# Attention's score and value products spaced on PE, and the first expert weights issued from GpSimd in 1 KB rows

## The chip, the cores and the metric

One core of a Trainium2 chip. The metric is the device time of one execution in microseconds; of several runs of a kernel the median counts. The engines are TensorE (PE in the profile, with its weight loads as PEld), VectorE (DVE), ScalarE (ACT), GpSimd (POOL) and SyncE (SP, which here only starts DMA transfers).

## The reference, cut to what matters

Chunked attention with memory slots over 4 batches, 8 heads, 768 positions and head size 64; its output, as 3072 tokens of 512 numbers, goes through a layer of 8 experts whose shares P come from a Sinkhorn iteration.

```python
# attention: chunk 32, left 16, right 8, 8 memory slots, scale 1/sqrt(64)
for c in range(nc):
    l_start, r_end = max(0, c_start - 16), min(S, c_end + 8)
    k_full = concatenate([mem_k, k[:, :, l_start:r_end]], axis=2)
    v_full = concatenate([mem_v, v[:, :, l_start:r_end]], axis=2)
    scores = scale * (q[:, :, c_start:c_end] @ k_full^T)
    a = exp(scores - max(scores))
    out[:, :, c_start:c_end] = (a / (sum(a) + 1e-9)) @ v_full

# experts: x is (3072, 512), w1[e] (512, 1024), w2[e] (1024, 512)
P = exp(x @ w_gate - max(x @ w_gate))
for _ in range(8):
    P /= P.sum(1, keepdims=True) + 1e-9
    P /= P.sum(0, keepdims=True) + 1e-9
    P *= N / E
for e in range(8):
    out += P[:, e:e+1] * (maximum(x @ w1[e], 0) @ w2[e])
```

## The kernel before

**Tiling.** Attention works on blocks of 128 queries, 24 in all; for a block n PE transposes queries and keys (tq, tk, and now and then tx for extra keys kx), makes the scores (`sp`, 64 small fp32 products), DVE takes their maximum (sm) and subtracts it (s), ACT takes the exponential, PE transposes it (ta) and makes the values product (`xp`, 64 small products again), DVE divides (rec, xq) and PE transposes the result into token columns (xt). Four blocks make a unit of 512 tokens; there are six units. `build(u)` turns a unit's tokens into operands for the experts.

The experts' products run in fp16 on numbers split into a high and a low half, three passes for each product. A scale comes first: the maximum of a weight tile or of the tokens (DVE, `most`, L540 and L956), reduced over the partitions by PE (row_w, sp_w, row_x, sp_x); then ACT writes the high half (L495) and DVE the low half (L503). Most products of expert and unit use a scheme with seven products in place of eight (L1580: px, py, pz and, for the second layer, yx, yy, yz). Unit 0 of expert 0 uses plain products: `pp` (L2017) for the first layer and `yp` (L2098) for the second, because only sums and splits of plain weights are needed for them, and so they come first on PE. They need the first weights w1f of expert 0, four tiles of 512 KB (fp = 0 to 3), and the tokens of blocks 0 to 3.

**The order of the work.** Nothing is issued where the Python stands. Every step is a `Task` with an engine, a cost in microseconds, a priority (small goes first) and its dependencies; a `Plan` then simulates all engines with these costs and takes, again and again, the task that can start earliest, and among those that could start already the one with the smallest priority number. The program of each engine is the order that comes out of it. Each transfer has a cost in that plan too: one clock `dma` for all queues, pushed on by the transfer's `dma` number. Where PE would stand still by the plan for more than 0.4 us, `pad` puts filler products into PE's program (L409, `warm`, a 128 x 256 product on the identity that nobody reads):

```python
if t.eng == "PE" and self.fill is not None and at - clock["PE"] > 0.4:
    self.pad(clock["PE"], at)
```

The priorities at the head of the program are numbers written by hand: `BLOCKS = (-50.0, -44.0, -30.0, -26.0)` for the four blocks of unit 0, `VALUES` for their values, and `FIRST = (-38.0, -20.0)` for the first layer's and the second layer's weights of expert 0. `fetch_first(1, START)` loads the four tiles of w1, takes their maxima and makes their scale; `plain1` splits them. All loads but a few of ACT are issued by SyncE (`eng="SP"`), one after the other, and a w1 tile is two of them (fh = 0 and 1), each of 256 KB in rows of 512 bytes:

```python
for fh in range(2):
    queue.dma_start(st.t[:, fh], w1v[e, fp, :, :, fh])
```

In `hidden()`, which makes the first layer by the scheme of seven products, every product waits for all pieces of its two operands (`made = wmade + xmade`).

Of the kernel before, what the change touches and what calls it, by code (L numbers as in the profile page):

```python
# [24 lines left out]
BEHIND = 5.0  # L25
FIRST = 2.0
MARGIN = 8.0
FAR = 60.0


class Task:


    __slots__ = ("eng", "cost", "fn", "prio", "left", "ready", "end", "then", "takes", "frees", "n", "dma", "start")
# [55 lines left out]
class Plan:  # L90
# [8 lines left out]
    def __init__(self):  # L99
        self.tasks = []  # L100
        self.free = {}
        self.fill = None

    def add(self, eng, cost, fn, deps=(), prio=0.0, bufs=(), takes=None, frees=None, dma=0.0):
        t = Task()
        t.eng, t.cost, t.fn, t.prio, t.takes, t.frees = eng, cost, fn, prio, takes, frees
        t.ready, t.end, t.then, t.n, t.dma = 0.0, None, [], len(self.tasks), dma
        if dma:
            t.cost = cost * ISSUE
# [23 lines left out]

    def run(self):
# [3 lines left out]
        dma = FIRST  # L138
# [4 lines left out]
        while left:  # L143
            best = None
            for e in self.ENGINES:
# [5 lines left out]
                pick = None  # L151
                for _, _, t in sorted(a):
                    if t.takes is None or self.free.get(t.takes.group):
                        at = now
                        if t.takes is not None:
                            at = max(at, self.free[t.takes.group][0][0])
                        if pick is None or at < pick[0]:
                            pick = (at, t, a)
                        if at <= now:
                            break  # L160
                for r, _, t in sorted(w)[:12]:
                    if pick is not None and r >= pick[0]:
                        break
                    if t.takes is None or self.free.get(t.takes.group):
                        at = r
                        if t.takes is not None:
                            at = max(at, self.free[t.takes.group][0][0])
                        if pick is None or at < pick[0]:
                            pick = (at, t, w)
# [15 lines left out]
            if t.dma:  # L185
                at = max(at, dma - BEHIND)
                t.start = at
                clock[t.eng] = at + t.cost
                dma = max(dma, at + t.cost / 2) + t.dma
                t.end = max(dma, at + t.cost) + 2.6  # L190
            else:
                clock[t.eng] = t.end = at + t.cost
            t.fn()
# [2106 lines left out]
```

## Time and profile before

| | us |
|---|---|
| median of 3 runs | 1922.85 |
| lowest and highest run | 1922.3 and 1923.82 |
| span of the profiled execution | 1921.2 |
| PE busy in it | 1905.9 |
| DVE, ACT and POOL busy in it | 1436.7, 1032.3 and 520.3 |

The profile is of one execution. A row of a timeline gives the start, the duration, the engine, the line, the operation, the tiles (out<-in) and how many instructions are taken together; the bracket at its end is the idle time of the engine just before, with what ended it. "issue" stands where an engine waited for nothing that the profile shows. PEclk is the granted clock of PE as a share of full speed: 1.00 is 2.4 GHz, 0.50 is 1.2 GHz. Rows of the views stand further down in numbered groups.

### The profile page before, as it was taken

What the parts mean: (1) busy time and instruction counts of PE and PEld (TensorE: products, weight loads), DVE (VectorE), ACT (ScalarE), POOL (GpSimd) and SP (SyncE); (2) the same over time, 40 slices, a digit from 0 to 9 for tenths busy, and PEclk for the clock granted to TensorE, in tenths of its full rate; (3) what the DMA queues carried; (4) which work ended last, traced back from release to release, by engine and by line L of the source; (5) the groups of instructions that cost most, each with busy time, mean ns of one, the idle gap of its engine ahead of it and who ended that gap; (6) DMA issues with size and microseconds to landing.
All of it is one profiled execution on the core that took longest, in us unless ns stands there. A gap on an engine that the chain in (4) does not pass through costs nothing.

```text
span 1921.2 us, 47293 instructions
## 1 busy us (share of the span) xinstructions
PE 1905.9 (99%) x19608; PEld 1641.5 (85%) x19608; DVE 1436.7 (75%) x2396; ACT 1032.3 (54%) x2019; POOL 520.3 (27%) x549
## 2 busy tenths in 40 slices
PE   8999999999999999999999999999999999999999
PEld 7676676688888888888888888888888888888888
DVE  5666569778769866897778875898678885786565
ACT  4665564556556545645545554654554564564453
POOL 1220002443224231432124231342124232332112
PEclk9999999999999999999999999999999999999999
DMA  8677653454235342255214533245313632322321
GB/s 197 174 202 205 169 162 122 138 176 144 83 103 173 131 138 94 78 178 186 109 57 148 204 105 127 78 160 171 143 45 99 242 128 92 102 83 83 127 83 67
DMA packets 246792, 254.82 MB, mean 133 GB/s; under 512 B 113265, under 2 KB 180273, under 8 KB 242225
## 3 DMA queue, kind: packets, MB, share of 16 engines
q1 hardware_dynamic: 244452, 251.21, 40.8%
q8 instruction: 153, 2.51, 0.5%
q10 hardware_dynamic: 2124, 0.59, 0.2%
q14 instruction: 63, 0.51, 0.1%
HBM read 187.84 MB, written 63.44 MB: 131 GB/s over the span
## 4 chain that ended last, share of the span: by engine, by line
PE 94%; DVE 3%; issue 1%; DMA 1%; ACT 0%; POOL 0%; SPq 0%; DVEq 0%; POOLq 0%
PE px L1580 26%; PE yx L1580 22%; PE pz L1580 13%; PE yz L1580 11%; PE py L1580 6%; PE yp L2098 6%; PE yy L1580 5%; PE xp L1119 1%; PE sp L1051 1%; PE pp L2017 1%; DVE ss L1738 1%; PE warm L409 1%; PE ta L1109 0%; PE tk L992 0%; PE tq L988 0%
## 5 line engine op out<-in xcount | busy, mean ns | idle before, releaser
L1580 PEld LDWEIGHTS <-w 128*128 128x128 f16 x7896 | 770.9, 98 | 93.1 <-issue 0.8
L1580 PEld LDWEIGHTS <-h 128*128 128x128 f16 x7056 | 689.9, 98 | 82.9 <-issue 2.6
L1580 PE MATMUL px<-x,w 128*128 128x256 f16 x4512 | 549.1, 273 | 0.5 <-issue 0.3
L1903 POOL TENSOR_TENSOR acc<-acc,y 128x256 f32<-128x256 f32 x252 | 265.6, 1060 | 862.4 <-ACT y L1878 839.8
L1580 PE MATMUL yx<-w,h 128*128 128x256 f16 x4032 | 467.6, 273 | 0.7 <-DVE acc L1913 0.6
L1629 ACT ACTIVATE q<-px 128x256 f32<-128x256 f32 x376 | 142.7, 381 | 304.4 <-PE px L1580 299.8
L1580 PE MATMUL pz<-x,w 128*128 128x256 f16 x2256 | 278.4, 273 | 0.0
L1580 PE MATMUL yz<-w,h 128*128 128x256 f16 x2016 | 233.8, 273 | 1.2 <-ACT y L1878 1.2
L1798 DVE TENSOR_TENSOR h<-ss,h 128x1024 f16<-128x1024 f32 x160 | 214.7, 1344 | 3.8 <-ACT h L1774 3.5
L1749 ACT ACTIVATE h<-c 128x768 f16<-128x768 f32 x168 | 140.8, 838 | 109.5 <-DVE c L1639 109.5
L1774 ACT CAST h<-ss 128x1024 f16<-128x1024 f32 x168 | 174.2, 1040 | 24.9 <-DVE ss L1738 24.0
L1738 DVE SCALAR_TENSOR_TENSOR ss<-c,ss 128x256 f32<-128x256 f32 x336 | 172.3, 513 | 8.2
L1782 DVE SCALAR_TENSOR_TENSOR h<-c,h 128x768 f16<-128x768 f32 x168 | 165.0, 982 | 11.2 <-ACT h L1749 11.2
L1639 DVE SCALAR_TENSOR_TENSOR c<-px,q 128x256 f32<-128x256 f32 x188 | 77.7, 421 | 94.2 <-PE px L1580 85.0
L1878 ACT ACTIVATE y<-yx,pscale 128x256 f32<-128x256 f32 x168 | 79.3, 473 | 112.6 <-PE yx L1580 108.8
L1580 PE MATMUL py<-x,w 128*128 128x256 f16 x1128 | 139.2, 273 | 0.0
L1639 DVE SCALAR_TENSOR_TENSOR c<-py,q 128x256 f32<-128x256 f32 x188 | 78.8, 422 | 72.1 <-PE py L1580 66.1
L2098 PE MATMUL yp<-w,h 128*128 128x512 f16 x576 | 131.7, 379 | 0.0
L1738 DVE SCALAR_TENSOR_TENSOR ss<-c,h 128x512 f32<-128x512 f32 x168 | 122.7, 730 | 2.2 <-ACT h L1726 2.2
L1580 PE MATMUL yy<-w,h 128*128 128x256 f16 x1008 | 116.9, 273 | 0.0
L2098 PEld LDWEIGHTS <-h 128*128 128x128 f16 x576 | 55.4, 98 | 58.9
L503 DVE SCALAR_TENSOR_TENSOR w<-ws,sw,w 128x1024 f16<-128x1024 f32 (+1 forms) x64 | 84.9, 1326 | 25.8 <-ACT w L495 25.8
(158 smaller groups left out, 1755.1 us busy)
## 6 DMA issues: line engine op xcount, KB each, us to landing
x<-xkeep SPq DMA_DIRECT2D x28, 1792.0 KB
akeep<-acc SPq DMA_DIRECT2D x168, 256.0 KB
acc<-akeep SPq DMA_DIRECT2D x168, 256.0 KB
w1f<-in_moe_w_dram SPq DMA_DIRECT2D x72, 256.0 KB
w2f<-in_moe_w_dram SPq DMA_DIRECT2D x32, 512.0 KB
w1fm<-in_moe_w_dram SPq DMA_DIRECT2D x56, 256.0 KB
w2fm<-in_moe_w_dram SPq DMA_DIRECT2D x28, 512.0 KB
xkeep<-x SPq DMA_DIRECT2D x6, 1792.0 KB
```

The source lines that it names most:

```text
L503: lambda: nc.vector.scalar_tensor_tensor(dst(1), src(), s, dst(0), op0=ALU.mult, op1=ALU.subtract),
L1580: nc.tensor.matmul(dst.t, a, b, start=(not more and n == 0), stop=(n == end), skip_group_check=more,)
L1629: lambda: nc.scalar.activation(t.t, src.t, AF.Copy, scale=DOWN),
L1639: lambda: nc.vector.scalar_tensor_tensor(c.t[:, o], src.t, DOWN, q.t, op0=ALU.mult, op1=ALU.add),
L1738: lambda: nc.vector.scalar_tensor_tensor(dst(), src(), 0.0, other(), op0=ALU.max, op1=op),
L1749: lambda: nc.scalar.activation(h.t[:, 0, 0:3], c.t, AF.Relu),
L1774: lambda: nc.scalar.copy(h.t[:, 0, 3:7], ss.t),
L1782: lambda: nc.vector.scalar_tensor_tensor(h.t[:, 1, 0:3].rearrange("p a n -> p (a n)"), c.t.rearrange("p a n -> p (a n)"), 0.0, h.t[:, 0, 0 ...
L1798: lambda: spare.tensor_tensor(h.t[:, 1, 3:7], ss.t, h.t[:, 0, 3:7], op=ALU.subtract),
L1878: (lambda: nc.scalar.activation(t.t, src.t, AF.Copy, scale=f))
L1903: lambda: nc.gpsimd.tensor_tensor(acc.t[:, cols], acc.t[:, cols], q.t, op=ALU.add),
L2098: nc.tensor.matmul(py.t, hf.t[:, hl, where[fh], o : o + P], room(fp, WIDE * wl + DM * fh, WIDE * wl + DM * (fh + 1)), start=(fp == 0 and i ...
```

## The change

Five things.

1. **Spacing.** The tasks of scores and values products from block 2 on are marked `many`. When one has been placed, the plan remembers its end plus 3.6 us (`again`). If the next pick on PE is such a task and would start before that, the plan takes another task in its place, if one could start no later than 0.1 us after it.
2. **First weights.** The four w1 tiles of expert 0 are issued by GpSimd, with priority -60 in place of -38, and their maxima and splits have earlier priorities. In the plan GpSimd's transfers have a clock of their own beside that of SyncE and ACT.
3. **Rows of 1 KB.** Every w1 tile is loaded as one transfer of 512 KB with rows of 256 numbers, in place of two with rows of 128. A tile holds other columns than before, so w2's rows are grouped to match, and the places inside the tiles follow (`place`, `source`, `tile1`).
4. **Block 1** has the priority -48 in place of -44 for its queries and keys.
5. **Waits in `hidden()`.** A product waits for the pieces of its operands that it reads.

The diff, cut:

```diff
+APART = 3.6
...
     def run(self):
...
-        dma = FIRST
+        dma = {"SP": FIRST, "POOL": FIRST}
...
+                pick = self.next(now, w, a, False)
+                if pick is not None and pick[1].many and pick[0] < self.again:
+                    other = self.next(now, w, a, True)
+                    if other is not None and other[0] <= pick[0] + 0.1:
+                        pick = other
...
             if t.dma:
-                at = max(at, dma - BEHIND)
+                own = "SP" if t.eng == "ACT" else t.eng
+                at = max(at, dma[own] - BEHIND)
...
+            if t.many:
+                self.again = t.end + APART
...
-    w1v = w1.rearrange("e (kt p) (fh fp f) -> e fp p kt fh f", p=P, fh=2, fp=FP)
-    w2v = w2.rearrange("e (fh fp p) d -> e fp p fh d", fh=2, fp=FP)
+    w1v = w1.rearrange("e (kt p) (fp f) -> e fp p kt f", p=P, fp=FP)
+    w2v = w2.rearrange("e (fp fh p) d -> e fp p fh d", fh=2, fp=FP)
...
-        queue = nc.scalar if eng == "ACT" else nc.sync
+        queue = {"ACT": nc.scalar, "POOL": nc.gpsimd, "SP": nc.sync}[eng]
...
-                for fh in range(2):
-                    queue.dma_start(st.t[:, fh], w1v[e, fp, :, :, fh])
+                queue.dma_start(st.t.rearrange("p k a f -> p k (a f)"), w1v[e, fp])
...
-        return st, add(eng, 2 if which == 1 else 1, go, after, prio, [st], dma=2.1)
+        return st, add(eng, 1, go, after, prio, [st], dma=2.1 if eng == "SP" else 2.8)
...
-    BLOCKS = (-50.0, -44.0, -30.0, -26.0)
+    BLOCKS = (-50.0, -48.0, -30.0, -26.0)
     VALUES = (-47.0, -41.0, -28.0, -24.0)
-    FIRST = (-38.0, -20.0)
+    FIRST = (-60.0, -20.0)
...
-        t = add("PE", 0.9, go, made + (after_v[1:2] if n == BU // 2 else []), at, [qT, kC, s], takes=sp)
+        t = add("PE", 0.9, go, made + (after_v[1:2] if n == BU // 2 else []), at, [qT, kC, s], takes=sp, many=n > 1)
...
-        t = add("PE", 0.9, go, [t] + lv, at + 2, [vt, aT], takes=xp)
+        t = add("PE", 0.9, go, [t] + lv, at + 2, [vt, aT], takes=xp, many=n > 1)
...
-        made = wmade + xmade
+        def made(op):
+            a, b = op
+            if e > 0:
+                of_w = wmade[0 if a < 2 else 1 if a == 2 else 2 :][:1]
+            else:
+                of_w = wmade[0 if a < 3 else 1 if a == 3 else 2 :][:1]
+            if len(xmade) != 8:
+                return of_w + xmade
+            i = (0, 2, 3, 1, 1, 1, 1)[b]
+            return of_w + [xmade[i], xmade[4 + i]]
...
-            st, ld = load(0, fp, which, FIRST[which - 1] + 0.5 * fp)
+            st, ld = load(
+                0, fp, which, FIRST[which - 1] + 0.5 * fp, eng="POOL" if which == 1 else "SP"
+            )
...
-    for fp, s in enumerate(fetch_first(1, START)):
-        plain1(fp, *s, START - 6.0 + 2.0 * fp)
+    for fp, s in enumerate(fetch_first(1, START - 10.0)):
+        plain1(fp, *s, START - 14.0 + 2.0 * fp)
```

What this does to the engines' programs shows at three places. DVE's program at its head, before the change; mxs is the maximum of a w1 tile, vmax one of values, sp and xp are attention's products:

```order
L732 MEMSET v_pair 128x32
L1062 MEMSET sp_301 32x2x4x16
L1065 TENSOR_REDUCE sm_339<-sp_301 128x2x4
L1071 TENSOR_TENSOR s_344<-sp_301,sm_339 128x2x4x64
L956 TENSOR_REDUCE vmax<-v_pair 128x1
L1137 TENSOR_SCALAR rec_427<-xp_389 128x8
L1138 RECIPROCAL rec_427<-rec_427 128x8
L1139 TENSOR_TENSOR xq_430<-xp_389,rec_427 128x2x4x64
```

and DVE's program at the same place with the change:

```order
L761 MEMSET v_pair 128x32
L558 TENSOR_REDUCE mxs<-w1f_0_163 128x1
L558 TENSOR_REDUCE mxs<-w1f_1_167 128x1
L558 TENSOR_REDUCE mxs<-w1f_2_177 128x1
L1091 MEMSET sp_308 32x2x4x16
L1094 TENSOR_REDUCE sm_359<-sp_308 128x2x4
L1100 TENSOR_TENSOR s_373<-sp_308,sm_359 128x2x4x64
L558 TENSOR_REDUCE mxs<-w1f_3_185 128x1
L446 TENSOR_REDUCE most_of<-mxs 128x1
L985 TENSOR_REDUCE vmax<-v_pair 128x1
```

Three maxima of the w1 tiles have moved ahead of the reading of block 0's scores, the fourth right behind it.

SyncE's program at its head, before the change: block 0's and block 1's queries and keys (q, k), extra keys (kx), values (v_pair), and the w1 tiles:

```order
L772 DMA kx_175<-in_k_dram 32x8x64
L903 DMA v_pair<-in_v_dram 16x4x64
L903 DMA v_pair<-in_v_dram 40x4x64
L903 DMA v_pair<-in_v_dram 56x4x64 x3
L830 DMA q_188<-in_q_dram 128x8x64
L827 DMA k_192<-in_k_dram 128x8x64
L772 DMA kx_175<-in_k_dram 32x8x64 x2
L903 DMA v_pair<-in_v_dram 56x4x64 x4
L531 DMA w1f_0_286<-in_moe_w_dram 128x4x128 x2
...
L830 DMA q_432<-in_q_dram 128x8x64
```

and with the change:

```order
L801 DMA kx_179<-in_k_dram 32x8x64
L859 DMA q_183<-in_q_dram 128x8x64
L856 DMA k_191<-in_k_dram 128x8x64
L801 DMA kx_179<-in_k_dram 32x8x64 x2
L932 DMA v_pair<-in_v_dram 16x4x64
L932 DMA v_pair<-in_v_dram 40x4x64
L932 DMA v_pair<-in_v_dram 56x4x64 x7
L859 DMA q_341<-in_q_dram 128x8x64
L856 DMA k_349<-in_k_dram 128x8x64
L551 DMA w2f_0_352<-in_moe_w_dram 128x2x512
```

The eight w1 transfers are gone from this queue (they stand in GpSimd's, behind gate's MEMSET), block 1's queries and keys stand ahead of the values, and block 2's (q_341, k_349) and the first w2 tile follow at once.

PE's program towards the end of unit 0's first layer, before the change, one scores and one values product with what stands between them; the rows left out are products of the same two kinds, twelve in all, each with its weight load:

```order
L1051 MATMUL sp_1580<-kC,qT_1547 32x64 x32
L1109 MATMUL ta_1618<-ident,s_1569 128x128 x4
L2017 LDWEIGHTS w_0_1_657
L2017 MATMUL pp_1_1_0_1625<-w_0_0_1097,w_0_1_657 128x256
...
L2017 MATMUL pp_1_1_0_1625<-x_626,w_0_1_657 128x256
L1119 MATMUL xp_1647<-x_room,at_1635 32x65 x32
```

and at the corresponding place with the change, where the rows left out are such products too, 24 in all:

```order
L1080 MATMUL sp_1606<-kC,qT_1482 32x64 x32
L2056 LDWEIGHTS w_0_2_564
L2056 MATMUL pp_1_2_0_1643<-w_0_0_1026,w_0_2_564 128x256
...
L817 MATMUL tx_1652<-ident,kx_1332 128x128 x4
L1017 MATMUL tq_1660<-ident,q_1317 128x128 x4
L1021 MATMUL tk_1670<-ident,k_1330 128x128 x4
...
L2056 MATMUL pp_1_3_1_1687<-x_699,w_0_3_604 128x256
L1148 MATMUL xp_1706<-x_room,at_1602 32x65 x32
```

The twelve ordinary products and one transposition between the two attention products have become 24 and three.

## Rows read from the trace of the kernel before

**Rows 1.** The page: its span, and busy time, share and instructions of each engine.

```profile
span 1921.2 us, 47293 instructions
...
PE 1905.9 (99%) x19608; PEld 1641.5 (85%) x19608; DVE 1436.7 (75%) x2396; ACT 1032.3 (54%) x2019; POOL 520.3 (27%) x549
```

**Rows 2.** Windows: stretch, length, busy per engine (count), clock, DMA share, GB/s.

```profile
0.00:34.00 34.00, 30.50 (x467) 24.70 (x468) 16.60 (x35) 14.13 (x26) 4.95 (x12) 1.00 0.84 183
34.00:110.00 76.00, 70.44 (x1298) 52.28 (x1296) 56.16 (x100) 51.03 (x102) 15.33 (x18) 0.96 0.76 189
...
290.00:1921.00 1631.00, 1626.07 (x14656) 1432.63 (x14654) 1250.13 (x2042) 860.59 (x1673) 481.04 (x495) 1.00 0.36 123
```

**Rows 3.** PE's timeline, 37 to 51 us: start, duration, operation.

```profile
37.43 2.13 PE L2017 MATMUL pp<-x,w 128*128 128x256 f16 x18
...
44.53 0.81 PE L1119 MATMUL xp<-w,at 64*32 64x65 f32 x58
47.18 0.31 PE L1119 MATMUL xp<-w,at 64*32 64x65 f32 x6 [1.83 <-issue]
...
47.53 3.67 PE L2017 MATMUL pp<-x,w 128*128 128x256 f16 x18
```

**Rows 4.** Windows, 48 to 50 us, same columns as rows 2.

```profile
48.00:50.00 2.00, 2.00 (x12) 1.40 (x10) 1.91 (x4) 0.05 (x1) 0.00 (x0) 0.50 0.52 118
```

**Rows 5.** PE's timeline, 76 to 90 us.

```profile
76.08 0.86 PE L1119 MATMUL xp<-x_room,at 64*32 64x65 f32 x64
...
85.85 0.86 PE L1119 MATMUL xp<-x_room,at 64*32 64x65 f32 x64
...
89.21 1.25 PE L2017 MATMUL pp<-w,w 128*128 128x256 f16 x5 [2.28 <-issue]
```

**Rows 6.** DMA queues: packets, MB, share of 16 engines' span.

```profile
q8 instruction: 153, 2.51, 0.5%
```

**Rows 7.** PE's timeline, 175 to 182 us.

```profile
175.74 0.86 PE L1119 MATMUL xp<-v_pair,at 64*32 64x65 f32 x64
...
180.56 0.34 PE L1119 MATMUL xp<-v_pair,at 64*32 64x65 f32 x16
181.22 0.72 PE L1119 MATMUL xp<-v_pair,at 64*32 64x65 f32 x48 [0.31 <-issue]
```

**Rows 8.** Timelines of DVE, SyncE's queue and PE, 14 to 35 us.

```profile
14.35 0.17 DVE L1062 MEMSET sp<- 32x128 f32 x1 [13.41 <-PE sp L1051]
14.55 5.38 SPq L531 DMA_DIRECT2D w1f<-in_moe_w_dram  x8
34.06 1.11 PE L2017 MATMUL pp<-x,w 128*128 128x256 f16 x6
```

**Rows 9.** DVE's timeline, 22 to 25 us.

```profile
22.48 2.33 DVE L540 TENSOR_REDUCE mxs<-w1f 128x1 f32<-128x1024 f32 x2
```

**Rows 10.** DVE by line, 14 to 34 us: tiles, count, busy us, mean ns, idle before.

```profile
L503 DVE SCALAR_TENSOR_TENSOR x<-xg,sx,x 128x512 f16<-128x512 f32 x2 | 1.5, 742 | 0.3 <-ACT x L495 0.3
...
L1071 DVE TENSOR_TENSOR s<-sp,sm 128x512 f32<-128x512 f32 x2 | 1.4, 691 | 0.1
...
L503 DVE SCALAR_TENSOR_TENSOR w<-w1f,sw,w 128x1024 f16<-128x1024 f32 x1 | 1.3, 1278 | 0.0
```

**Rows 11.** PE by line and shape, same columns, whole span.

```profile
L409 PE MATMUL warm<-ident 128*128 128x256 bf16 x160 | 22.2, 296 | 1.6 <-POOL ident masks.py:199 1.6
```

**Rows 12.** The chain of waits, 0 to 60 us: start, duration, what.

```profile
10.68 1.20 PE warm L409 x11
...
36.72 0.44 PE tq L988 x4
```

**Rows 13.** Timelines of PE and DVE, 94 to 108 us.

```profile
94.83 0.86 PE L1119 MATMUL xp<-v_pair,at 64*32 64x65 f32 x64
105.41 1.67 DVE L503 SCALAR_TENSOR_TENSOR x<-xg,sx,x 128x256 f16<-128x256 f32 x4
```

**Rows 14.** The chain of waits, 340 to 400 us.

```profile
363.12 20.72 PE yp L2098 x96
```

More of the change, by code (lines that the diff above doesn't have):

```diff
@@ L27 @@
 MARGIN = 8.0
+APART = 3.6
 FAR = 60.0
 class Task:
-    __slots__ = ("eng", "cost", "fn", "prio", "left", "ready", "end", "then", "takes", "frees", "n", "dma", "start")
+    __slots__ = ("eng", "cost", "fn", "prio", "left", "ready", "end", "then", "takes", "frees", "n", "dma", "start", "many")
 class Past:
@@ L102, in __init__, with add @@
         self.fill = None
-    def add(self, eng, cost, fn, deps=(), prio=0.0, bufs=(), takes=None, frees=None, dma=0.0):
+        self.again = 0.0
+    def add(self, eng, cost, fn, deps=(), prio=0.0, bufs=(), takes=None, frees=None, dma=0.0, many=False):
         t = Task()
@@ L107, in add @@
         t.ready, t.end, t.then, t.n, t.dma = 0.0, None, [], len(self.tasks), dma
+        t.many = many
         if dma:
@@ L132, in pad, with next @@
                 return
+    def next(self, now, w, a, spread):
+        pick = None
+        for _, _, t in sorted(a):
+            if spread and t.many:
+                continue
+            if t.takes is None or self.free.get(t.takes.group):
+                at = now
+                if t.takes is not None:
+                    at = max(at, self.free[t.takes.group][0][0])
+                if pick is None or at < pick[0]:
+                    pick = (at, t, a)
+                if at <= now:
+                    break
+        for r, _, t in sorted(w)[:12]:
+            if spread and t.many:
+                continue
+            if pick is not None and r >= pick[0]:
+                break
+            if t.takes is None or self.free.get(t.takes.group):
+                at = r
+                if t.takes is not None:
+                    at = max(at, self.free[t.takes.group][0][0])
+                if pick is None or at < pick[0]:
+                    pick = (at, t, w)
+        return pick
     def run(self):
@@ L518, in load @@
     def load(e, fp, which, prio, ahead="", eng="SP", after=()):
-        shape = [P, 2, KT, P] if which == 1 else [P, 2, DM]
+        shape = [P, KT, 2, P] if which == 1 else [P, 2, DM]
         place = "stage", stage
@@ L1654, in hidden @@
         px, py, pz = psum("px"), psum("py"), psum("pz")
-        t1 = run(px, P1, False, made, px)
+        t1 = run(px, P1, False, [], px)
         q1, r1 = read(px, "q1", t1)
```

57 lines of the change are left out of this document (23 added, 34 removed).

## The prediction

> **What bounds the kernel now.** I read the busy table first [rows 1]: TensorE (PE) is busy 1905.9 of 1921.2 us, so only a change of what PE does, or of how long it stands still, can move the end. The table of stages [rows 2] says where that could be: from 290 us on PE is busy 1626.07 of 1631 us with the transfers at a 0.36 share, before that PE is idle for 3.5 us up to 34 us and for 5.6 us between 34 and 110 us, where the granted clock is 0.96. So everything this change can give lies in the first 300 us.
>
> The PE rows in order of time then show what the 34 to 110 us stretch loses. At 47.18 us a values product goes on after 1.83 us of waiting for nothing that the trace names, and the 18 products behind it take 3.67 us where the 18 at 37.43 us took 2.13 [rows 3]. In those microseconds the granted clock is 0.50, the lower level of 1.2 GHz, after PE had stood still [rows 4]. The same happens at 89.21 us: 2.28 us of nothing, then the slow stretch [rows 5]. What is PE waiting for? The queue that brings instructions moved 2.51 MB in 153 packets [rows 6], 16.4 KB each; PE runs 19608 products and as many weight loads [rows 1], 39216 in all, and 39216 / 153 = 256 per packet. An attention product (scores sp, values xp) is 64 small products with 64 weight loads, 128 instructions in 0.86 us, half a packet [rows 5]; 18 ordinary products take 2.13 us for 36 [rows 3]. My reading: where several attention products stand close together PE uses up its instructions faster than packets come through the loaded DMA engines. Ahead of the second stop four of them start between 76.08 and 85.85 us [rows 5], 3.3 us apart on average.
>
> What those stops cost: 1.83 + 2.28 us of standing still, twice 3.67 - 2.13 = 1.54 us of slow clock, and 0.31 us in a smaller one at 181.22 us [rows 7]: 7.5 us together.
>
> **The products kept apart.** The planner only writes another order; no instruction and no wait is added by it. In the new order at least 3.1 us of other work lie between an attention product's end and the next one's start in the stretch that was 34 to 110 us, 4.0 us or more from start to start, against the 3.3 us in front of the second stop. Does that remove the stops? Bounds: all 7.5 us gone, or all of them back. Rows for the middle: at 181.22 us PE stopped although the products had started 4.82 us apart (175.74 and 180.56), wider than the narrowest new spacing; but it stopped for 0.31 us only [rows 7]. So I expect shorter and fewer stops, not none, and take half: 3.75 us saved. What is bought with it: the same attention work is spread over more of unit 0, so block 7's values come later relative to unit 0's own products (below).
>
> **The first weights from GpSimd.** Before, SyncE issues them as eight transfers from 14.55 us on, 5.38 us of issuing [rows 8]; now GpSimd issues four right after its first four small operations. The maxima of these tiles move in VectorE's (DVE) queue: three of the four, 1.2 us each [rows 9], now stand ahead of block 0's scores, in time where DVE sat idle 13.41 us [rows 8]. So if the third tile has landed by about 13.1 us (14.35 less one maximum) they cost nothing. The first hidden products then wait for DVE's chain in the new order: from block 0's scores at 14.35 us to the second split of the tokens, four weight splits (4 x 1.28), two value maxima and two weight maxima (4 x 1.2), two blocks' scores (4 x 0.69), two blocks' division (2 x 1.06, its large operation 0.69 like the scores'), two token splits (2 x 0.74) and some 2.2 us of small ones: 18.5 us, with 0.5 us waiting for block 1's scores and the first of the two token splits being enough to start, 32.7 us [rows 8, 10]. PE itself, with 15 fillers in front, gets there at about 33.1. Before it was 34.06 [rows 8]: 1.0 us sooner.
>
> That is not 1.0 us saved. PE runs 160 filler products before [rows 11] and 159 in the new order, at 1.20 us for 11 of them, 0.11 each [rows 12]: so PE's whole time changes only by what it stands still and by the clock. Up to the first hidden product the new order has 129 fillers instead of 157 (28 x 0.11 = 3.1 us less) and three more pieces of attention, one scores product (0.86) and two transposes (0.44 each) [rows 5, 12], 1.7 us more. PE stands still 3.1 - 1.7 - 1.0 = 0.4 us more.
>
> The other fillers come back where unit 1 begins: 25 in front of its first px and 5 behind, 3.2 us, where three stood before. They cover the wait for unit 1's tokens. In the trace of before block 7's values product starts at 94.83 us, and the last of the four token splits of the row at 105.41 us ends 12.25 us after it [rows 13]. In the new order PE has, from that product on, 24 yp (96 take 20.72 us [rows 14], so 5.2), one xp and one sp (1.7), five transposes (2.2), the gate logits and some small ones (put at 1.5) and 25 fillers (2.7): 13.3 us. So the tokens are there about when PE is; I put 0.4 us of standing still on it, between 0 and 1.5.
>
> **Where the loads collide.** The 2 MB now start near 2 us instead of 14.55, among block 0's and block 1's queries, keys and values. No row has a transfer issued from GpSimd. Bounds for the delay of the third tile behind 13.1 us: none, if the four share the engines evenly from 2 us on (the 34 us ahead have a DMA share of 0.84 [rows 2], so there is some room, not much); and 9 us, if they land as late as before, when DVE's first read of them started at 22.48 us [rows 9]. I take 1.0 us, near the lower end, because that read came eight microseconds after the first issue and the issue is now twelve earlier: the first maximum could start near 10 us, the third 2.4 us later.
>
> The Trainium skill, "DMA: Bandwidth & Descriptors", section "Issuing engines are not separate DMA queues", speaks against this part: transfers started from several engines run on the same 16 DMA engines and interleave, and only the issuer's time is saved. By that rule alone SyncE's 5.38 us would be the gain and the loads would slow each other, which is rival C below; no run here shows a transfer from GpSimd.
>
> **At no cost.** Rows of 1 KB for all of w1: fewer, larger packets in a stage where PE does not wait for transfers [rows 2]; cover gone, a late tile would hold PE's weights. Block 1's queries and keys three transfers sooner: its scores product gains some 0.4 us, inside DVE's chain above. The other order of w1's columns and w2's rows, and a product waiting for the pieces of its operands that it reads: same sizes, no wait that is longer. GpSimd's four copies behind the loads wait for block 0's values anyway.
>
> **The sum.** 1921.2 - 3.75 + 0.4 + 0.4 + 1.0 = 1919.25 us for the profiled span. The span lies 1.65 us under the median of 1922.85, so 1920.9 us.
>
> **The rivals.** (B) The stops vanish: all 7.5 us come back, the tiles land in time: 1922.85 - 7.5 + 0.4 = 1915.75, about 1916. For it: both long stops have the tightest groups of products. Against: the stop at 181.22 us. (C) Slower, one mechanism: the loads from GpSimd land late, among the transfers that SyncE has under way. DVE stands at the maximum of the third tile with block 0's scores queued behind it, ACT's exponential and PE behind those; every microsecond after 13.1 is one at the end, and above 3 us it eats what I forecast. At the far bound, 9 us instead of 1: 1920.9 + 8 = 1929. (D) The change doesn't do what it says: packets are late because the DMA engines are loaded, whatever the spacing, and 7.5 us of stops come back at other places: 1922.85 + 1.8 = 1924.7.
>
> **How the numbers follow.** My forecast, 1920.9 with a range of its own of 1919 to 1922.5, has 0.45; B 0.33; C 0.13; D 0.09. A run of this kernel can tell about 0.2%, 3.85 us, from no change: faster is below 1919.0, slower above 1926.7. B is faster, and 0.03 of my own case; C slower but for 0.02 of it; the rest within. Faster 0.36, same 0.53, slower 0.11. For the range I reach from just under B to 1926, over D, and leave C's far part out: 1914.5 to 1926.
>
> **What would show it.** Right: in the PE rows up to 300 us stops "for nothing" adding up to some 2 to 5 us with at most one stretch at clock 0.50; the first hidden product near 33 us with DVE's second token split just ahead; some 25 fillers where unit 1 begins and no long wait behind them; the first maximum on DVE before 10 us and the third ended by 15. Wrong: block 0's scores read on DVE clearly after 15 us (C); PE waiting for token splits after the fillers of unit 1 (the spreading costs more than I put on it); no stop at all (B), or stops of 2 us and both slow stretches with the wider spacing (D).

## The result and the profile after

The changed kernel takes 1929.88 us (median of 5 runs, 1929.17 to 1932.44) against 1923.26 for the kernel before: 1.0039 times as long, 95% interval 1.0029 to 1.0050. It is slower by some 7 us (6.6 by the medians, 7.5 by the ratio). The forecast was 1920.9, and the range ended at 1926.0.

The page of the changed kernel, the lines that answer to [rows 1], and the stages as in [rows 2]:

```profile
span 1928.1 us, 47150 instructions
...
PE 1906.6 (99%) x19607; PEld 1642.1 (85%) x19607; DVE 1435.5 (74%) x2396; ACT 1033.6 (54%) x2019; POOL 526.2 (27%) x553
```

```profile
0.00:34.00 34.00, 26.11 (x411) 20.25 (x412) 15.21 (x26) 12.38 (x23) 8.28 (x16) 0.90 0.83 194
34.00:110.00 76.00, 68.54 (x1279) 51.17 (x1277) 51.99 (x93) 50.07 (x99) 17.22 (x21) 0.99 0.74 178
...
290.00:1928.00 1638.00, 1631.94 (x14722) 1437.86 (x14719) 1252.60 (x2051) 864.76 (x1679) 484.11 (x495) 1.00 0.36 124
```

PE is as busy as before, within 0.7 us, and stands still for 21.5 us in place of 15.3 (span less busy time). What it stood still for shows in PE's timeline of the changed kernel; the bracket is the idle time just before the row:

```profile
15.21 0.43 PE L817 MATMUL tx<-ident,kx 64*128 64x64 f32 x4 [3.50 <-DMA kx<-in_k_dram]
19.22 1.18 PE L1080 MATMUL sp<-kC,qT 64*32 64x64 f32 x64 [2.38 <-ACT kC L1038]
...
39.70 2.78 PE L2056 MATMUL pp<-x,w 128*128 128x256 f16 x24
...
46.93 0.66 PE L1017 MATMUL tq<-ident,q 128*128 128x128 f32 x4 [0.49 <-DMA q<-in_q_dram]
...
57.18 0.63 PE L1017 MATMUL tq<-ident,q 128*128 128x128 f32 x4 [1.64 <-DMA q<-in_q_dram]
...
88.16 0.66 PE L1080 MATMUL sp<-kC,qT 64*32 64x64 f32 x41 [0.59 <-issue]
...
94.47 0.34 PE L1148 MATMUL xp<-x_room,at 64*32 64x65 f32 x15 [0.78 <-issue]
...
107.01 0.66 PE L1017 MATMUL tq<-ident,q 128*128 128x128 f32 x4 [3.04 <-DMA q<-in_q_dram]
...
108.04 0.66 PE L1021 MATMUL tk<-ident,k 128*128 128x128 f32 x4 [0.37 <-DMA k<-in_k_dram]
```

Four things are to be seen. The waits for "issue" ([rows 3], [rows 5], [rows 7]) are down from 4.76 us (1.83, 2.28, 0.31 and a fourth of 0.34) to 1.37, and neither of the two that are left is followed by slow products. PE waits 5.88 us (3.50 and 2.38) for block 0's keys and for what ACT makes of them, where before it waited for neither. The first hidden product comes at 39.70 us, not at 34.06 [rows 8]. And later there are 5.54 us of waits for queries and keys (0.49, 1.64, 3.04, 0.37) that were not there either. 5.88 + 5.54 - 3.39 is 8.03 us; the difference in standing still is 6.2, so all other waits together have lost 1.8.

That PE is as busy as before hides a fifth thing. The two stretches at clock 0.50 behind the long stops are gone, some 3 us of busy time [rows 3], but there are two new ones behind the new waits, from about 17 to 24 us (the clock of 0.90 in the first stage above) and from 109 to 113 us:

```profile
20.00:22.00 2.00, 2.00 (x37) 1.59 (x24) 1.44 (x3) 0.79 (x2) 0.00 (x0) 0.50 0.60 84
110.00:112.00 2.00, 2.00 (x6) 0.68 (x5) 0.00 (x0) 0.00 (x0) 0.00 (x0) 0.50 0.78 215
```

Block 0's 64 scores products take 1.18 us in the first of them (the row at 19.22), against 0.86 for 64 such products at clock 1.00 [rows 5]. So these two waits cost more than their own length.

Why are block 0's keys late? DVE's timeline of the changed kernel shows that the tiles from GpSimd were not:

```profile
8.38 1.22 DVE L558 TENSOR_REDUCE mxs<-w1f 128x1 f32<-128x1024 f32 x1 [7.43 <-DMA w1f<-in_moe_w_dram]
10.95 1.22 DVE L558 TENSOR_REDUCE mxs<-w1f 128x1 f32<-128x1024 f32 x1 [1.35 <-DMA w1f<-in_moe_w_dram]
12.51 1.22 DVE L558 TENSOR_REDUCE mxs<-w1f 128x1 f32<-128x1024 f32 x1 [0.34 <-DMA w1f<-in_moe_w_dram]
20.49 0.17 DVE L1091 MEMSET sp<- 32x128 f32 x1 [6.76 <-PE sp L1080]
```

The third maximum ends at 13.73 us; then DVE waits 6.76 us for block 0's scores. The DMA queues between 5 and 10 us (packets, MB, share of the 16 engines; q1 is SyncE's, q10 ScalarE's, q0 GpSimd's), before:

```profile
q10 hardware_dynamic: 1440, 0.38, 44.2%
q1 hardware_dynamic: 1027, 0.24, 25.9%
```

and in the changed kernel:

```profile
q0 software_dynamic: 327, 1.22, 78.5%
q10 hardware_dynamic: 578, 0.14, 16.5%
q1 hardware_dynamic: 490, 0.12, 12.7%
```

GpSimd's 2 MB go in packets of 3.7 KB on average (1.22 MB / 327; 297 of them have 4096 bytes, the others 4) and hold the DMA engines for eight tenths of the time; the other two queues move 0.26 MB where they moved 0.62. Behind that the issuing queues themselves stand still, as the timelines of ScalarE's and SyncE's queues show. Before:

```profile
1.69 5.74 ACTq L903 DMA_DIRECT2D v_pair<-in_v_dram  x9
9.13 1.28 ACT L1016 ACT_TABLE_LOAD   x1 [9.13 <-DMA v_pair<-in_v_dram]
```

```profile
10.03 0.43 SPq L830 DMA_DIRECT2D q<-in_q_dram  x1
```

In the changed kernel:

```profile
1.68 8.62 ACTq L932 DMA_DIRECT2D v_pair<-in_v_dram  x9
14.12 1.57 ACTq L919 DMA_DIRECT2D v_pair<-v_pair  x2
15.71 1.28 ACT L1045 ACT_TABLE_LOAD   x1 [15.71 <-DMA v_pair<-in_v_dram]
```

```profile
9.10 0.32 SPq L801 DMA_DIRECT2D kx<-in_k_dram  x1
14.26 0.40 SPq L859 DMA_DIRECT2D q<-in_q_dram  x1
```

ScalarE issues block 0's values itself; that took 5.74 us before and takes 8.62 now, then it waits until 14.12 for them to land, and only then does its other work begin, with a table load at 15.71 us, against 9.13 before; the copies that make kC come behind it. SyncE issues block 1's queries at 14.26 us, before at 10.03, although they stand further ahead in its program.

### The profile page after: what moved, and what is told of

It reads as the page before. It is cut to its first block, busy times and chain, and to the rows that moved or that the text cites. A ratio compares the mean times of both kernels' runs of the same rounds, so it can differ in the third digit from the quotient of the medians.

```text
span 1928.1 us, 47150 instructions
## 1 busy us (share of the span) xinstructions
PE 1906.6 (99%) x19607; PEld 1642.1 (85%) x19607; DVE 1435.5 (74%) x2396; ACT 1033.6 (54%) x2019; POOL 526.2 (27%) x553
## 4 chain that ended last, share of the span: by engine, by line
PE 95%; DMA 2%; SPq 1%; DVE 1%; issue 0%; POOL 0%; ACT 0%; ACTq 0%; DVEq 0%; POOLq 0%
PE px L1609 26%; PE yx L1609 23%; PE pz L1609 13%; PE yz L1609 11%; PE py L1609 6%; PE yp L2137 6%; PE yy L1609 6%; PE sp L1080 1%; PE xp L1148 1%; DMA kx<-in_k_dram 1%; PE tq L1017 0%; DMA xkeep<-x 0%; SPq L932 0%; PE tk L1021 0%; PE xt L1189 0%
## 5 line engine op out<-in xcount | busy, mean ns | idle before, releaser
L514 ACT ACTIVATE w<-ws,sw 128x1024 f16<-128x1024 f32 (+1 forms) x64 | 69.3, 1088 | 67.1 <-POOL ws L602 67.0
```

The lines of the kernel that those rows point to most:

```text
L514: lambda: nc.scalar.activation(dst(0), src(), AF.Copy, scale=s),
```

## The experiments

Ratios are to the kernel before, measured on the same chip in the same job, with their 95% intervals. They compare between jobs better than the medians do: the kernel before itself had medians from 1921.7 to 1923.3 us.

**Each half by itself.** The first two kernels have the spacing alone, and everything but the spacing.

```diff
# spacing_alone: the kernel before, with this part of the change only
+APART = 3.6
...
+                if pick is not None and pick[1].many and pick[0] < self.again:
...
# no_spacing: the changed kernel
-APART = 3.6
+APART = 0.0
```

> The kernel before with the spacing of the attention products as its only edit; its program has 174 fillers where before had 160, 1.5 us more. Theory 1 (the early transfers from GpSimd hold up the first queries, keys and values, and the spacing by itself saves time): the two long stops and both slow-clock stretches go, 6 to 7 us, less 1.5 for fillers: 1917 to 1919 us, first hidden product at 34 us. Theory 2 (the spacing is what costs, by pushing the queries of later blocks against other transfers): 1924 us or more, with PE waiting for DMA of q at about 55 and 105 us.

Measured: 1919.44 us, 0.9985 (0.9977 to 0.9994). Theory 1's mechanism, with less of its gain: its stops for "issue" come to 0.23 us in one place, the clock is 1.00 in all four stages, but 3.0 us of waits for queries, keys and gate weights are new, and there are 14 fillers more (1.5 us). 7.5 - 0.2 - 3.0 - 1.5 is 2.8 us, about what was measured.

> The changed kernel with the spacing set to 0; 129 fillers in place of 159, 3.3 us less. Theory 1: the first 40 us stay as they are in the changed kernel (PE waits some 3.5 us for kx and 2.4 us for kC), the stops for instructions come back (+5 to +7), fillers give 3.3 back: 1931 to 1934 us. Theory 2: the waits for q go and the time is 1926 or less.

Measured: 1925.64 us, 1.0023 (1.0013 to 1.0032). A miss for theory 1: without the spacing the changed kernel is no slower, rather faster. Its stops came to 2.38 us (1.54 and 0.84) and no slow stretch followed them, so there was only 1.0 us to win over the 1.37 of the changed kernel, and the spacing pays 30 fillers, 3.3 us, for it. (The profiled execution, 1930.44 us, was one of the longer ones of 1923.1 to 1934.4, so these stops may not be those of the median.) What spacing is worth depends on what stands around it; the series below shows the other end.

**Is it the 2 MB?**

```diff
# quarter_loads: the changed kernel
-                queue.dma_start(st.t.rearrange("p k a f -> p k (a f)"), w1v[e, fp])
+                nc.gpsimd.memset(st.t[:, 1:KT], 0.0)
+                queue.dma_start(st.t[:, 0].rearrange("p a f -> p (a f)"), w1v[e, fp][:, 0])
...
# sp_first: the changed kernel
-    FIRST = (-60.0, -20.0)
+    FIRST = (-38.0, -20.0)
...
-                0, fp, which, FIRST[which - 1] + 0.5 * fp, eng="POOL" if which == 1 else "SP"
+                0, fp, which, FIRST[which - 1] + 0.5 * fp, eng="SP"
...
+    for fp, s in enumerate(fetch_first(1, START)):
+        plain1(fp, *s, START - 6.0 + 2.0 * fp)
```

> The changed kernel, same order on PE and DVE, but GpSimd loads only a quarter of each of the four first w1 tiles (0.5 MB in place of 2) and fills the rest with zeros, so that quarter of the weights alone enters unit 0's first layer. Theory 1 (what is carried early crowds out the first keys): kx no longer waited for or by under 1 us, ACT's first activation back to about 10.5 us, first hidden product at 33 to 34.5 us, time 1920 to 1923. Theory 3 (the order of SyncE's queue, with block 1's keys ahead, is what delays block 0): 1928 or more, kx still waited for by 3 us.

Measured: 1921.46 us, 0.9998 (0.9989 to 1.0007). With a quarter of the bytes, and the same order on PE and DVE, the wait for kx is gone. Three rows of PE's timeline in this kernel:

```profile
13.68 0.86 PE L1083 MATMUL sp<-kC,qT 64*32 64x64 f32 x64 [1.38 <-ACT kC L1041]
...
22.68 0.66 PE L1020 MATMUL tq<-ident,q 128*128 128x128 f32 x4 [2.37 <-DMA q<-in_q_dram]
...
98.07 0.66 PE L1020 MATMUL tq<-ident,q 128*128 128x128 f32 x4 [3.03 <-DMA q<-in_q_dram]
```

Block 0's scores start at 13.68 us and not at 19.22. That is theory 1, and against theory 3. The edit changes more than the bytes, though: the filling with zeros stands ahead of each transfer on GpSimd, so the four are issued from 2.31 to 6.8 us and not from 1.62 to 4.9. And two waits for queries are left: 2.37 us for block 2's, and the 3 us near 100 us, which so do not need the 2 MB.

> The changed kernel with the first weights issued by SyncE again, with their earlier priorities of the kernel before; spacing, 1 KB rows, block 1's earlier keys and the narrower waits stay. Theory 1: no wait for kx, first hidden product at 33.5 to 34.5 us, stops mostly gone: 1917 to 1919 us. Theory 3: kx still late, 1926 or more.

Measured: 1918.53 us, 0.9982 (0.9974 to 0.9991), the lowest median here, though not parted from spacing_alone's. PE waits for neither kx nor kC, stops come to 1.75 us, the granted clock is 1.00 throughout the first 300 us, the first hidden product is at 34.55. So what makes the changed kernel slow is in the second of the five things, the first weights: their queue, their clock in the plan and their priorities.

**The same kernel again, and the size of the packets.**

```diff
# packets_1k: each tile as four transfers, one for each kt
+                    for j in range(KT):
+                        queue.dma_start(
+                            st.t[:, j].rearrange("p a f -> p (a f)"), w1v[e, fp][:, j]
+                        )
...
# packets_4k: each tile as four transfers, 32 partitions each
+                    for j in range(4):
+                        r = slice(32 * j, 32 * j + 32)
+                        queue.dma_start(
+                            st.t[r].rearrange("p k a f -> p k (a f)"), w1v[e, fp][r]
+                        )
```

> The changed kernel itself once more, beside the next three on one chip: 6 to 8 us above the kernel before.

Measured: 1927.41 us, 1.0035 (1.0023 to 1.0047). 5.5 us above the kernel before by the medians, 6.7 by the ratio: the same finding.

> The changed kernel with each first w1 tile issued by GpSimd as four transfers, one for each of the four rows of 1 KB that a partition gets; same order on PE and DVE. Theory 1a (a DMA engine takes one packet from each queue in turn, so GpSimd's packets of 4 KB, 171 ns each, take eight tenths of its time from packets of 256 B, 18 ns): packets of 1 KB, about 46 ns, take some 46 / (46 + 18 + 18) = 0.56, kx and values land earlier, PE's wait for kx 0 to 2 us in place of 3.5, time 3 to 6 us under the changed kernel's. Theory 1b (it is the 2 MB that count, whatever the packets): no different from the next kernel, which has the same number of transfers.

> The changed kernel with each first w1 tile issued by GpSimd as four transfers of 32 partitions each, packets still 4 KB: as many transfers of the same size as the kernel with 1 KB packets, so the same pace of issuing. Theory 1a: like the changed kernel, PE waits 2.5 to 3.5 us for kx, time within 2 us of it. Theory 1b: like the kernel with 1 KB packets.

Measured: 1928.05 us, 1.0039 (1.0027 to 1.0051) for packets_1k, 1932.73 us, 1.0054 (1.0042 to 1.0066) for packets_4k. The pair does not test what it was made for, because the edit did not change the packets. GpSimd's queue over the whole execution, first in packets_1k, then in packets_4k:

```profile
q0 software_dynamic: 768, 2.10, 0.4%
```

```profile
q0 software_dynamic: 768, 2.10, 0.5%
```

In both, as in the changed kernel, 512 of these packets have 4096 bytes and the others 4: a transfer that takes one row of 1 KB for each partition still goes in packets of 4 KB. So nothing here decides between theories 1a and 1b, and what the size of the packets does stays open. What the pair does differ in is the part of a tile that one transfer carries. PE's wait for kx, first in packets_1k, then in packets_4k:

```profile
13.30 0.43 PE L823 MATMUL tx<-ident,kx 64*128 64x64 f32 x4 [2.31 <-DMA kx<-in_k_dram]
```

```profile
15.29 0.66 PE L824 MATMUL tx<-ident,kx 64*128 64x64 f32 x4 [4.36 <-DMA kx<-in_k_dram]
```

The queues from 10 to 14 us, in the same order:

```profile
q0 software_dynamic: 234, 0.63, 56.3%
q1 hardware_dynamic: 835, 0.21, 27.9%
```

```profile
q0 software_dynamic: 213, 0.57, 63.8%
...
q1 hardware_dynamic: 284, 0.07, 8.9%
```

With packets of the same size SyncE's queue gets through three times as much in packets_1k, and kx lands 2 us sooner; why is open. Both forecasts by theory 1a missed: packets_1k was to be 3 to 6 us under the changed kernel and is no faster, packets_4k within 2 us of it and is 4 to 5 us slower. (Of packets_4k the longest of its five executions was profiled; it has one stop of 3.17 us for "issue" at 138.41 us.) Sixteen transfers take GpSimd until 13 us to issue, and in packets_1k DVE now stands at the third tile's maximum until 15.72 us, the place that rival C named:

```profile
15.72 1.22 DVE L564 TENSOR_REDUCE mxs<-w1f 128x1 f32<-128x1024 f32 x1 [2.33 <-DMA w1f<-in_moe_w_dram]
```

Block 0's scores start at 15.19 us there, 4 us sooner than in the changed kernel, and yet the first hidden product comes at 39.16, only 0.5 us sooner. The late tiles and waits of 2.1 us for block 1's queries and keys stand in between; how much each took was not parted.

**Early, or only issued by GpSimd?** The next kernel holds GpSimd's transfers until block 1's keys have landed, in the changed kernel's plan; the two after it start from sp_first and change neither PE's, ACT's nor DVE's order.

```diff
# held: the changed kernel; the plan puts the first transfer behind the load of block 1's keys
+            if eng == "POOL" and fp == 0:
+                nc.gpsimd.tensor_copy(seen, state[1][1].t[:, 0, 0:1])
...
# gpsimd_early: sp_first, planned on SyncE, but written into GpSimd's program
-                queue.dma_start(st.t.rearrange("p k a f -> p k (a f)"), w1v[e, fp])
+                (nc.gpsimd if first else queue).dma_start(
+                    st.t.rearrange("p k a f -> p k (a f)"), w1v[e, fp]
+                )
...
# gpsimd_held: gpsimd_early, and ahead of the first of the four
+                    nc.gpsimd.tensor_copy(seen, state[1][1].t[:, 0, 0:1])
```

> The changed kernel in which GpSimd copies one column of block 1's keys before it issues the first weights, so these start only when those keys have landed, at some 14 us; the plan knows of it. Theory 1 (block 0 and 1 only have to come first; GpSimd as issuer is harmless): no wait for kx or kC over 1 us, first hidden product at 33 to 36 us, 1917 to 1922 us. Rival (transfers from GpSimd are harmful at any time, since they now push aside values and block 2's keys): 1926 us or more, with PE waiting over 3 us for values or queries between 20 and 60 us.

Measured: 1928.28 us, 1.0037 (1.0025 to 1.0049): the rival. Block 0 and 1 are on time, and block 2's queries pay, in PE's timeline of this kernel:

```profile
27.40 1.12 PE L1028 MATMUL tq<-ident,q 128*128 128x128 f32 x4 [7.55 <-DMA q<-in_q_dram]
```

They were issued at 16.09 us, two microseconds after GpSimd had begun to issue its transfers. A stretch at clock 0.50, from 23 to 34 us, lies around that wait.

> The kernel with the first weights issued by SyncE again, all its orders on PE, ACT and DVE unchanged, but the four transfers moved into GpSimd's program, where nothing holds them: they start at about 1.6 us. Theory 1 (the early 2 MB crowd out block 0's loads): PE waits 3 to 4 us for kx and 1 to 3 us for what follows, first hidden product 4 to 6 us later than in the kernel it is made from, time 1922 to 1926. Rival (the loss comes from the plan, which gives GpSimd's transfers a clock of their own and so plans SyncE's too tightly): within 2 us of 1918.5.

Measured: 1922.64 us, 0.9996 (0.9987 to 1.0005). Theory 1: with every order on PE, ACT and DVE kept, the move alone costs 0.14% by the ratios, each good to 0.09%, some 3 to 4 us over sp_first. PE's waits are those of the changed kernel, and so is a stretch at clock 0.50, from 16 to 24 us, that sp_first does not have:

```profile
14.60 0.43 PE L822 MATMUL tx<-ident,kx 64*128 64x64 f32 x4 [3.15 <-DMA kx<-in_k_dram]
...
18.64 1.19 PE L1085 MATMUL sp<-kC,qT 64*32 64x64 f32 x64 [2.40 <-ACT kC L1043]
```

No wait for queries over 0.2 us follows in it.

> As the last one, but GpSimd first copies one column of block 1's keys, so the four transfers start when those have landed, at about 14 us; orders on PE, ACT and DVE unchanged. Theory 1: block 0 and 1 are not late any more, wait for kx under 0.5 us. If it matters only who issues first, 1917 to 1920 us. If transfers from GpSimd push aside whatever SyncE has under way, now the values of blocks 0 and 1 and block 2's queries and keys, PE waits for values or for block 2's queries by 2 us or more: 1922 or more.

Measured: 1922.07 us, 0.9995 (0.9986 to 1.0004). This stays open. The time is above sp_first's, but the profiled execution was one of its fastest (1919.01 us) and shows no wait for values or queries over 0.2 us, only two stops for "issue", of 1.33 us at 24.22 us, with a stretch at clock 0.50 behind it, and of 0.53 us at 169.06. The time fits the second forecast, the waits do not. As no run issues the tiles early from SyncE, it is not shown whether the early start alone costs the 0.14% or GpSimd as the issuer has a part in it.

**The plan around it.** gpsimd_early leaves about 0.4% to the changed kernel. Either the plan's separate clock for GpSimd's transfers costs that, or the earlier maxima and splits.

```diff
# old_priorities: the changed kernel (GpSimd, clock of its own)
-    FIRST = (-60.0, -20.0)
+    FIRST = (-38.0, -20.0)
...
+    for fp, s in enumerate(fetch_first(1, START)):
+        plain1(fp, *s, START - 6.0 + 2.0 * fp)
...
# sp_early_maxima: sp_first
+    for fp, s in enumerate(fetch_first(1, START - 10.0)):
+        plain1(fp, *s, START - 14.0 + 2.0 * fp)
```

> The changed kernel with the first weights still issued by GpSimd and planned on a clock of their own, but with the priorities that loads, maxima and splits had before. SyncE's program keeps the changed kernel's order at its head (block 2's queries, then a w2 tile, then block 3's). If the separate clock costs the 5 us: 1925 to 1930 us, with waits for queries or keys of 2 us or more together at 45 to 60 and at 100 to 110 us. If the early maxima and splits do: 1921 to 1924 us.

Measured: 1923.11 us, 1.0007 (0.9998 to 1.0016). Without the early priorities the changed kernel is 0.28% faster (1.0007 against 1.0035 in after_again), so they make up most of what gpsimd_early left. PE has no wait for queries or keys between 58 and 350 us. But that is not where the time was won. PE stands still for 21.5 us in this profiled execution (span 1922.3 us), exactly as long as in the changed kernel, because 5.7 us of stops for "issue" stand where the waits were, in spite of the spacing of 3.6 us; the longest:

```profile
36.35 0.27 PE L1021 MATMUL tk<-ident,k 128*128 128x128 f32 x1 [2.29 <-issue]
```

The difference is in PE's busy time, 1900.8 us in place of 1906.6: 129 fillers in place of 159 (3.3 us), and one stretch at clock 0.50 in place of two. The early priorities cost 0.28% through the whole order that the plan makes of them, and no run takes that order apart.

> The kernel with the first weights issued by SyncE on the one clock, with the early priorities of maxima and splits put back. If the separate clock costs the 5 us: within 1.5 us of 1918.5, waits for queries under 1 us together. If the early maxima and splits do: 1922 to 1925 us.

Measured: 1921.75 us, 1.0006 (0.9996 to 1.0016); runs from 1918.4 to 1927.1. On SyncE and one clock the early maxima and splits (the loads keep -38 here) cost 0.24% against sp_first. The profiled execution was a long one (1926.9) and shows one place: the maxima stand ahead of block 1's division on DVE, so PE waits for it. It also has 3.1 us of stops for "issue", where sp_first has 1.75, a wait of 2.0 us for the gate's logits, where sp_first has 1.05, and two stretches at clock 0.50, where sp_first has none; the share of the maxima in the 0.24% is not shown.

```profile
27.18 0.66 PE L1189 MATMUL xt<-ident,xq 128*128 128x128 f32 x4 [2.66 <-DVE xq L1168]
```

The separate clock by itself, old_priorities against gpsimd_early, is 0.11%, which the two intervals of 0.09% each way do not part from nothing.

**How far apart?** The spacing of sp_first, 3.6 us, against three others:

```diff
# sp_first_0, sp_first_2, sp_first_5: sp_first
-APART = 3.6
+APART = 0.0   # 2.4 and 5.0 in the other two
```

> The kernel with the first weights issued by SyncE, with the spacing set to 0: what is left is 1 KB rows, block 1's earlier keys and the narrower waits. 186 fillers where that kernel has 163, 2.5 us more. If the spacing is what gains: stops for nothing of 4 us or more together and one or two slow-clock stretches, 1922 to 1926 us. If the other parts gain: 1919 or less.

> The kernel with the first weights issued by SyncE, spacing 2.4 in place of 3.6 us; 166 fillers. If stops depend on how many attention products stand within some microseconds: stops of 1 to 4 us together, 1919 to 1922 us; if 2.4 is enough: 1918 or less.

> The kernel with the first weights issued by SyncE, spacing 5.0 in place of 3.6 us; 245 fillers in place of 163, 9 us more. If stops are all that counts: as fast as with 3.6, 1917 to 1919 us. If the plan pays for the spacing with fillers that stand where PE has no other work: 1924 to 1929 us.

| spacing | median, us | ratio (95%) | stops for "issue", us | fillers |
|---|---|---|---|---|
| 0 | 1929.32 | 1.0030 (1.0018 to 1.0041) | 5.50 | 186 |
| 2.4 | 1924.76 | 1.0010 (1.0001 to 1.0019) | 5.14 | 166 |
| 3.6 | 1918.53 | 0.9982 (0.9974 to 0.9991) | 1.75 | 163 |
| 5.0 | 1947.16 | 1.0130 (1.0116 to 1.0144) | 0.21 | 245 |

With 2.4 the two long stops are still there, in PE's timeline of that kernel:

```profile
47.50 0.30 PE L1148 MATMUL xp<-w,at 64*32 64x65 f32 x4 [1.77 <-issue]
...
90.33 0.30 PE L1148 MATMUL xp<-x_room,at 64*32 64x65 f32 x3 [2.60 <-issue]
```

With 3.6 they are gone in sp_first (the largest left is 0.78 us). With 5.0 attention itself ends too late: from 290 to 352 us PE is busy 51.84 of 62 us, where before it was busy for all of them, and waits for the routing's small operations, which need the last unit's logits; from 335 to 352 us the granted clock is 0.51:

```profile
337.15 0.60 PE L1545 MATMUL cp<-cs,one 128*128 128x8 f32 x2 [3.31 <-DVE cs L1517]
...
344.26 0.60 PE L1545 MATMUL cp<-cs,one 128*128 128x8 f32 x2 [3.16 <-DVE cs L1517]
```

All three are over what was expected: sp_first_0 (1922 to 1926), sp_first_2 (1919 to 1922, with stops of 1 to 4 us) and, by far, sp_first_5. sp_first_0 has the rows of 1 KB, block 1's earlier keys and the narrower waits without the spacing and without GpSimd, and is 0.30% slower than the kernel before: those three were not free in every order.

## Why the prediction was wrong, point by point

**The stops.** Right in kind, too small in size. The prediction took half of 7.5 us. In the changed kernel 1.37 us of standing still for "issue" are left of 4.76, with no slow stretch behind them, 6.5 us less; in spacing_alone and sp_first it is much the same. Two things limit this. In the changed kernel most of that is not the spacing's: without it (no_spacing) the stops come to 2.38 us, also with no slow stretch behind them. And the spacing does not keep long stops away by itself: with 3.6 us there are stops of 2.29 us in old_priorities, 2.43 in sp_early_maxima and 3.17 in packets_4k. So the spacing of the products is not all that decides on a long stop, and the small stop at 181.22 us [rows 7], on which "half" rested, says nothing of their size either way. Nor does a slow stretch follow every long stop: in sp_first_0, with stops of 1.84 and 2.86 us, the clock stays at 1.00.

That PE was waiting for its instructions was argued from the number of packets [rows 6]. The traces' record of single packets bears it out. In the kernel before, q8, the queue that brings them, starts a packet at 44.46 us that takes 1.23, and PE goes on at 47.18; it starts one at 86.75 us that takes 1.01, and PE goes on at 89.21. Of the 35 stops for "issue" of 0.2 us or more up to 350 us in all profiles of this case, 34 end 1.2 to 1.8 us after such a packet has ended, while the packets come some 7 us apart. Why a packet comes late when it does (the loaded DMA engines, as the prediction had it, or something else) is not shown; the two just named were under way for no longer than the others up to 200 us (0.9 to 1.4 us).

**The first weights.** Here the prediction failed. The step is the term of 1.0 us under "Where the loads collide": it asked when the third w1 tile would land and bounded that, 0 to 9 us. The tile landed on time: its maximum started at 12.51 us, before the 13.1 allowed, so that term was nothing. The collision fell on the other side, for which the sum had no term. Block 0's keys and values, on the same 16 engines in packets of 256 B, were late beside GpSimd's; PE stood still for 5.88 us and ran at clock 0.50 from about 17 to 24 us; block 0's scores moved from 13.40 to 19.22 us and the first hidden product from 34.06 to 39.70, where 33.1 was forecast. The DMA share of 0.84 in the first 34 us [rows 2] was read as "some room". It should have been read the other way: the work of the first 15 us waits for transfers, so what moves ahead pushes those back. The price of the move can be read off one pair, gpsimd_early against sp_first, at 3 to 4 us.

The Trainium skill, "DMA: Bandwidth & Descriptors", section "Issuing engines are not separate DMA queues", was named in the prediction and held: the share that GpSimd's queue took, 78.5%, came out of the others'. The same page, section "Queues, rings and completion order", says that an engine goes round its queues and takes a whole packet from one before it turns to the next; that would give the queue with the larger packets the larger share. The trace agrees in direction, with 78.5% for 327 packets of 3.7 KB against 29.2% for 1068 of some 256 B in those five microseconds; equal turns it does not show (327, 578 and 490 packets), and no run changed the size of the packets.

**Rival C** named 1929, close to the 1929.88 measured, but by luck: its mechanism, a third tile 8 us later than in the forecast, with DVE standing at its maximum, did not happen. It was right in kind, in that the loads slow each other, and wrong in which is slowed; a third tile that holds DVE up shows only in packets_1k. The sign that the prediction named for it, block 0's scores read on DVE clearly after 15 us, did come (at 20.49 us), by the other road: one sign served two mechanisms. Its 0.13 was too little: it was priced as one late tile, and every load of the first 15 us was a candidate.

**Block 1's queries and keys "at no cost".** The gain of 0.4 us did not come: they were issued at 14.26 us instead of 10.03, because SyncE's queue stood still in front of them. PE did not wait for them in the changed kernel, as block 0 was later still.

**Fillers and unit 1.** Right. Two rows of PE's and one of DVE's timeline in the changed kernel:

```profile
119.76 2.67 PE L428 MATMUL warm<-ident 128*128 128x256 bf16 x23
122.27 1.47 PE L1609 MATMUL px<-x,w 128*128 128x256 f16 x12
120.98 1.67 DVE L522 SCALAR_TENSOR_TENSOR x<-xg,sx,x 128x256 f16<-128x256 f32 x4
```

25 fillers stand in front of unit 1's first px, which starts without waiting. What the step missed comes fifteen microseconds ahead of it: SyncE's queue in the changed kernel,

```profile
88.94 0.35 SPq L1267 DMA_DIRECT2D xkeep<-x  x1
89.34 9.23 SPq L932 DMA_DIRECT2D v_pair<-in_v_dram  x8
...
101.22 0.37 SPq L859 DMA_DIRECT2D q<-in_q_dram  x1
```

where a transfer of 1.8 MB stands directly in front of eight for values, and block 9's queries behind them; PE waits 3.04 us for these, and the clock is at 0.50 behind that. That order comes with the early priorities: the wait (with its neighbour on the keys, 0.9 to 3.4 us) is in every kernel here that has them on GpSimd, and in none of the others is there one of over 0.25 us between 98 and 108 us. The sum had no term for what the early maxima and splits move in SyncE's program 90 us later. But old_priorities, without this wait, stands still as long at other places, so the wait is where the early priorities show and not a measure of their 0.24 to 0.28%.

**The sum.** From sp_first (0.9982) to the changed kernel (1.0035 and 1.0039) are 0.53 to 0.57%, some 10 us. 0.14% is the move to GpSimd with orders kept, 0.24 to 0.28% the early priorities; the rest, up to 0.2%, was not parted further, and the separate clock may hold some of it. That the first weights as a whole are the cause is shown; of what the priorities do, only the size.

## What to carry to other kernels

A load that is issued from another queue and sooner may, as here, arrive instead of the others and not beside them: list every transfer that is under way in the stretch it moves into, and who waits for each, before asking when it lands itself. Look at the granted clock behind each new wait, and count the packets of a kernel that was made to change them. Spreading work to spare a starved engine had a best distance among the four tried in one plan (3.6 us), and did not pay in another; and a planner's order that is touched at its head should be read at its far end too.

## What was not expected of the hardware

A transfer that GpSimd issued moved in packets of 4 KB although its rows in memory are 1 KB (512 packets of 4096 bytes in the changed kernel), even where it took only one such row for each partition (packets_1k), while SyncE's queue in sp_first, with the same rows in it, counts 4091 packets for 2.54 MB between 14 and 24 us, too many for packets of 4 KB. GpSimd issued eight transfers of 128 KB without waiting and then waited for one to land before it went on, with one, two or four at a time (packets_1k, from 6.64 us on). And where a DMA queue is held up, the engine that issues from it is held up as well: ScalarE's nine issues took 8.62 us in place of 5.74, and its other work began 6.6 us later.
